# The last store moved to ScalarE's queue, and five stores in the middle halved

## The chip, the cores and the metric

The kernel runs on one core of one Trainium2 chip. The core has a matrix engine (TensorE, PE in the profile, with its weight loads shown as PEld), a vector engine (VectorE, DVE), an activation engine (ScalarE, ACT), GpSimd (POOL) and SyncE (SP), which here only issues transfers and waits. 16 DMA engines move data between the chip's memory (DRAM) and the core's on-chip memory (SBUF). The metric is the device time in microseconds (us) of one execution. It is given as the median of several executions; a profile is one execution more, with its own span from the first to the last instruction.

## The reference

Two stages, in float32. The first is attention through 32 inducing points, the second a two-branch expert with a maximum:

```python
B, N, m, C = (4, 12544, 32, 128)            # x: (B, N, C), inducing: (m, C)

def mab(q, kv):
    s = scale * (q @ kv.transpose(0, 2, 1))  # scale = 1/sqrt(C)
    s = s - s.max(-1, keepdims=True)
    a = np.exp(s)
    a /= a.sum(-1, keepdims=True) + 1e-09
    return a @ kv
h = mab(I, x)            # I: inducing for each batch; h: (B, m, C)
attn = mab(x, h)         # (B, N, C)

x = attn.reshape(B * N, 128)
h1 = x @ w1              # 128 -> 1024
h2 = x @ w2
g = np.maximum(h1, h2)
out = g @ w_out          # 1024 -> 128, (50176, 128)
```

## The kernel before

**Tiling.** A batch has 12,544 rows: 98 chunks of 128. The chunks are dealt into blocks of four quarters, a quarter being up to four chunks of one batch. A block is staged once (`stage`, L577): scores against the pooled `h`, then an exponential on ScalarE into a tile `e2`. For each quarter, "units" follow (`phase`, L990): a product of `e2` with `hwd`, which already holds `h` times the difference of the two weight matrices, and a ReLU of the result on ScalarE (L1006) or VectorE (L1009) into a relu tile. max(h1, h2) is h1 + relu(h2 - h1); the h1 part is added as a linear term (L786 for the quarters marked `full`, L990 for the others). A "group" is the output of one quarter: `final_one` (L797) runs eight products per chunk with `woutp` (L809), all into one PSUM bank.

**The output.** When the products of a group are done, `evict_group` (L826) scales them on VectorE by the softmax's reciprocal sums (L836) into an SBUF tile `osb`, shown as `o` in the profile, one of five buffers of the pool `outp`. It then stores the tile. There are 108 groups and 108 stores, each of one run of up to four neighbouring chunks: 90 of 256 KB, the others of 192, 128 and 64 KB. Before the change SP issues all of them (L861). The last four groups have four, three, two and one chunks, so the last store is 64 KB (128 partitions of 512 bytes).

**Other work on SP's queue.** Beside the three loads at the start, SP issues the transposing transfers of `x` (L171, tile `xT`) and of the pooling weights (L345, tile `eT`) of the next batches, in the same queue and between the stores. `xT` is read by L308, L330 and L591, `eT` by L364. SP takes its instructions in order: one that waits holds all that follow.

**What sets the order.** The Python code writes every instruction of every engine by hand: a clock model in the build (`Clock`, L20) decides at which step which work goes into the queues, and the framework keeps this order.

**Semaphores.** The framework gives the transfers issued from SP or ScalarE one of eight DMA semaphores in turn (index 0 to 7). Every such transfer first waits until the one eight before it, the former user of its index, has landed. SP issues 171 transfers in all, so the last store has index 2. A transfer adds to its semaphore 16 times; it has landed when the last of them is seen. When the last instruction has been written, the framework adds the closing of the program, which the profile shows under line 1200: SP waits in nine instructions, each for two semaphores at most, then in a drain. In the program's order the first is for two semaphores of GpSimd's transfers, the next eight are for DMA indices 0, 1, 2, 3, 4, 5, 6 and 7, each paired with another engine's semaphore, and the drain is for GpSimd's own. Then all engines meet at a barrier, twice, and the program ends. ScalarE issues no transfer before the change.

Of the kernel before, what the change touches and what calls it, by code (L numbers as in the profile page):

```python
# [102 lines left out]
def kernel(  # L103
# [9 lines left out]
    nc = tc.nc  # L113
# [23 lines left out]
    outr = out.rearrange("(b p k) c -> b p k c", b=B, p=128)  # L137
# [59 lines left out]
    with tc.manual_schedule(engines={ET.PE, ET.DVE, ET.Activation, ET.Pool, ET.SP}):  # L197
# [471 lines left out]
        for i in range(4):  # L669
# [3 lines left out]
            if i == 0:  # L673
# [5 lines left out]
                for dst, f in ((rep32, DOWN / scale), (repd, 1.0)):  # L679
                    nc.vector.tensor_scalar(  # L680
                        out=dst.rearrange("p (k m) -> p k m", m=M),
# [34 lines left out]
        groups, ends = [], [0] * 4  # L716
# [5 lines left out]
        groups = [g for _, _, g in sorted(groups, key=lambda e: e[:2])]  # L722
# [55 lines left out]
        def linear_last(end):  # L778

            while held:  # L780
                g = held[0]
                if g.full:
                    if st[g.blk.b].get("m1r", INF) > ck.pe:
                        return
                    for s, (q, t) in enumerate(g.chunks):
                        nc.tensor.matmul(  # L786
                            out=g.ps[:, 128 * s : 128 * (s + 1)],
                            lhsT=g.blk.e2[:, 128 * t : 128 * (t + 1)],
                            rhs=m1bd[:, q, :],
                            start=False,  # L790
                            stop=True,
                            skip_group_check=True,
                        )
                    end = ck.run(0.056 * len(g.chunks))
                evict_group(held.pop(0), end)
# [30 lines left out]
        def evict_group(g, end):  # L826
            n = len(g.chunks)
            uid[0] += 1
            osb = outp.tile([128, 4, C], F32, name=f"o_{uid[0]}", tag="o")
            qs = sorted({q for q, _ in g.chunks})  # L830
            per = n // len(qs)
            t0 = g.chunks[0][1]
            rp = g.blk.rp[:, t0 : t0 + per, qs[0] : qs[-1] + 1]
            if len(qs) == 1:
                rp = rp.broadcast_to((128, per, C))
                nc.vector.tensor_mul(osb[:, 0:n, :], g.ps[:, 0 : n * C].rearrange("p (s c) -> p s c", s=n), rp)  # L836
            elif per == 1:
                rp = g.blk.rp[:, t0, qs[0] : qs[-1] + 1]
                nc.vector.tensor_mul(
                    osb[:, 0:n, :],  # L840
                    g.ps[:, 0 : n * C].rearrange("p (s c) -> p s c", s=n),
                    rp[:, :, None].broadcast_to((128, n, C)),
                )
            else:
                for i, q in enumerate(qs):
                    nc.vector.tensor_mul(
                        osb[:, per * i : per * (i + 1), :],
                        g.ps[:, per * i * C : per * (i + 1) * C].rearrange("p (s c) -> p s c", s=per),
                        g.blk.rp[:, t0 : t0 + per, q : q + 1].broadcast_to((128, per, C)),
                    )  # L850
            ck.bank[g.bank] = ck.on_dve(end, 0.066 + n * 128 / 960.0)
            runs = []
            for s, (q, t) in enumerate(g.chunks):
                qu = g.blk.quarters[q]
                c = qu.c0 + t
                if runs and runs[-1][0] == qu.b and runs[-1][1] + runs[-1][3] == c:
                    runs[-1][3] += 1
                else:
                    runs.append([qu.b, c, s, 1])
            for b, c, s, m in runs:  # L860
                nc.sync.dma_start(out=outr[b, :, c : c + m, :], in_=osb[:, s : s + m, :])  # L861
            chunks_done[0] += n

        def finals_left():
# [159 lines left out]
        for b in range(1, B):  # L1024
            base = DONE0[b - 1]
            t_first, t_step = (6, 2.2) if b == 1 else (-6, 3.4)
            for u in range(NU):
                if b == 1:
                    s, turn, acc = 25 + 5 * u, 45 + 1.5 * u, 55 + 2 * u
                else:  # L1030
                    s = turn = 13 + 8.2 * u
# [5 lines left out]
            s, end = int(s), base + int(acc)  # L1037
# [167 lines left out]
```

## Time and profile before

| what | value |
|---|---|
| time, median of 3 runs | 327.31 us (327.06 to 327.68) |
| span of the profiled execution | 325.6 us (325.64 to the ns) |
| median less span | 1.67 us |
| granted TensorE clock | 1.000 |
| busy PE, DVE, ACT, POOL | 319.8, 283.1, 281.7, 25.6 us |
| DMA packets, bytes | 70,823, 53.65 MB |
| queue 1 (hardware, SP's) | 64,656 packets, 38.63 MB |

The span is the time from the first to the last instruction that the profile shows. Some time lies around it in the runs, here 1.67 us. A busy TensorE is the sum of its pipelined instructions, so its share says that it hardly pauses, not that it could go no faster. The chain that ended last is followed back from the last instruction: at each step to what released it. DMA-issuing instructions and waits on a queue are marked with a q (SPq, ACTq) and are not counted as busy. Where a line is said to be "of the trace's records", it is one instruction's own start and end, with more digits than the views print.

### The profile page before, as it was taken

The numbers are of one execution on the slowest core, as the hardware profiler recorded it, in microseconds if no ns is written. First come the engines' busy times: TensorE is split into PE (matmuls) and PEld (weight loads), VectorE is DVE, ScalarE is ACT, GpSimd is POOL, SyncE is SP. The second block draws the span as 40 slices with busy tenths as digits, with TensorE's granted clock in tenths as the row PEclk, the third lists the DMA queues.
The fourth block names the chain that finished last, engine by engine and source line by source line (L and its number), as shares of the span: only waits on it lengthen the run. The fifth ranks groups of instructions, "written<-read, shape, count | busy, mean of one in ns | idle before, by whom it ended". The sixth has DMA issues, their size and how long they took to land.

```text
span 325.6 us, 12570 instructions
## 1 busy us (share of the span) xinstructions
PE 319.8 (98%) x5404; PEld 243.0 (75%) x5404; DVE 283.1 (87%) x509; ACT 281.7 (87%) x560; POOL 25.6 (8%) x51
## 2 busy tenths in 40 slices
PE   7999999999999999999999999999999999999996
PEld 3876777777767777777777777777777777778785
DVE  3359989989989998998989999998989999999973
ACT  3679899999989899998888999989969999999961
POOL 7452030000040000000040000000000000000000
PEclk9999999999999999999999999999999999999999
DMA  8999999976279999993389999992312312222233
GB/s 204 208 206 214 286 246 212 172 207 134 97 150 245 225 248 209 201 203 86 116 162 243 214 234 232 190 192 86 115 66 101 113 68 98 90 108 99 85 115 112
DMA packets 70823, 53.65 MB, mean 165 GB/s; under 512 B 52176, under 2 KB 55408, under 8 KB 70768
## 3 DMA queue, kind: packets, MB, share of 16 engines
q1 hardware_dynamic: 64656, 38.63, 49.2%
q0 software_dynamic: 6112, 14.22, 22.3%
q8 instruction: 42, 0.69, 0.9%
q14 instruction: 13, 0.11, 0.1%
HBM read 28.33 MB, written 25.69 MB: 166 GB/s over the span
## 4 chain that ended last, share of the span: by engine, by line
PE 95%; DVE 1%; DMA 1%; ACT 0%; issue 0%; ACTq 0%; DVEq 0%
PE ps L809 61%; PE ps L990 22%; PE ps L591 2%; PE ps L232 2%; PE ps L308 2%; PE ps L364 1%; DMA xf<-in_x_dram 1%; PE ps L248 1%; DVE relu L1009 1%; PE ps L280 1%; PE ps L641 1%; PE ps L766 1%; PE ps L271 1%; PE ps L657 0%; PE ps L473 0%; PE ps L409 0%
## 5 line engine op out<-in xcount | busy, mean ns | idle before, releaser
L1006 ACT ACTIVATE relu<-ps 128x512 f16<-128x512 f32 x461 | 244.8, 602 | 26.6 <-PE ps L990 18.1
L1009 DVE TENSOR_SCALAR relu<-ps 128x512 f16<-128x512 f32 x323 | 206.8, 682 | 16.9 <-PE ps L990 15.3
L809 PE MATMUL ps<-woutp,relu 128*128 128x128 f16 x3136 | 217.3, 220 | 0.0
L809 PEld LDWEIGHTS <-relu 128*128 128x128 f16 x3136 | 176.7, 98 | 39.6 <-issue 29.1
L990 PE MATMUL ps<-e,hwd 32*128 32x512 f16 (+2 forms) x880 | 88.7, 360 | 0.0
L836 DVE TENSOR_TENSOR o<-ps,rp 128x512 f32<-128x512 f32 (+3 forms) x108 | 68.5, 634 | 5.5 <-PE ps L809 3.4
L990 PEld LDWEIGHTS <-hwd 32*128 32x128 f16 x880 | 24.9, 91 | 21.1 <-issue 1.0
L990 PE MATMUL ps<-m,e 32*128 32x128 f16 x381 | 38.8, 217 | 0.0
L990 PEld LDWEIGHTS <-e 32*128 32x128 f16 x381 | 21.3, 93 | 2.6
L165 POOL DMA_DIRECT2D xn<-in_x_dram x31 | 17.0, 557 | 8.2 <-DMA xn<-in_x_dram 4.3
L236 DVE COPY xT<-ps 128x512 f16<-128x512 f16 (+3 forms) x11 | 5.5, 504 | 7.8 <-PE ps L232 7.7
L319 ACT ACTIVATE eu<-ps 128x512 f16<-128x512 f32 x18 | 10.8, 615 | 0.0
L603 ACT ACTIVATE e<-ps 128x512 f16<-128x512 f32 (+2 forms) x21 | 10.5, 577 | 0.0
L164 POOL COPY pace<-hacc 128x1 f32<-128x1 f32 x2 | 0.4, 184 | 114.8 <-DVE hacc L397 114.8
L591 PE MATMUL ps<-xT,hT 128*32 128x512 f16 (+3 forms) x114 | 8.9, 362 | 0.0
L239 ACT COPY xT<-ps 128x768 f16<-128x768 f16 (+3 forms) x11 | 6.1, 556 | 2.7 <-PE ps L232 2.6
L232 PE MATMUL ps<-identity,xn 128*128 128x128 f16 x98 | 7.4, 219 | 0.4 <-DVE xn L661 0.3
L232 PEld LDWEIGHTS <-xn 128*128 128x128 f16 x98 | 5.6, 97 | 1.6 <-DVE xn L661 1.1
L257 ACT ACTIVATE et<-ps 128x448 f16<-128x448 f32 (+4 forms) x11 | 4.5, 413 | 2.6 <-PE ps L248 2.6
L308 PE MATMUL ps<-xT,inducingT 128*32 128x512 f16 x72 | 6.5, 385 | 0.0
L591 PEld LDWEIGHTS <-hT 128*32 128x32 f16 x114 | 3.3, 94 | 4.1 <-issue 3.0
L364 PE MATMUL ps<-xn,eT 128*32 128x128 f16 x288 | 5.5, 220 | 0.0
(96 smaller groups left out, 108.2 us busy)
## 6 DMA issues: line engine op xcount, KB each, us to landing
out_dram<-o SPq DMA_DIRECT2D x90, 256.0 KB, 2.4
xn<-in_x_dram POOLq DMA_DIRECT2D x24, 448.0 KB, 11.8
out_dram<-o SPq DMA_DIRECT2D x10, 128.0 KB, 3.0
xn<-in_moe_w_dram POOLq DMA_DIRECT2D x4, 256.0 KB, 14.1
xn<-in_x_dram POOLq DMA_DIRECT2D x4, 224.0 KB, 10.2
xT<-xn SPq DMA_TRANSPOSE x42, 4.3
xf<-in_x_dram SPq DMA_DIRECT2D x1, 512.0 KB, 3.9
xf<-in_x_dram SPq DMA_DIRECT2D x1, 384.0 KB, 4.3
```

The source lines that it names most:

```text
L165: nc.gpsimd.dma_start(out=xn_at[b, i][:, 0:n, :], in_=xr[b, :, k0 : k0 + n, :])
L232: nc.tensor.transpose(ps[:, j, :], xn[:, g + j, :], identity16)
L308: nc.tensor.matmul(out=ps[32 * g : 32 * (g + 1), :], lhsT=inducingT, rhs=xT_tiles[b % 2][:, U * u + 4 * g : U * u + 4 * (g + 1), :], start ...
L319: nc.scalar.activation(out=eu, in_=ps, func=AF.Exp, scale=scale, accum_out=st[b]["es"][:, u : u + 1])
L364: nc.tensor.matmul(out=ps[32 * g : 32 * (g + 1), 0:128], lhsT=eT[:, j, 32 * g : 32 * (g + 1)], rhs=xn_of(b, U * v + 4 * g + j), start=(j = ...
L591: nc.tensor.matmul(out=ps[32 * q : 32 * (q + 1), 128 * t : 128 * (t + n)], lhsT=hq, rhs=xT[:, c : c + n, :], start=True, stop=True, tile_p ...
L603: nc.scalar.activation(out=blk.e2[:, 0 : 128 * wd], in_=ps[:, 0 : 128 * wd], func=AF.Exp, scale=st[0]["rs"] if blk.b == 0 else scale,)
L809: nc.tensor.matmul(out=g.ps[:, 128 * c : 128 * (c + 1)], lhsT=g.blk.relu[q][:, 128 * (jb * w4 + t) : 128 * (jb * w4 + t + 1)], rhs=woutp[: ...
L836: nc.vector.tensor_mul(osb[:, 0:n, :], g.ps[:, 0 : n * C].rearrange("p (s c) -> p s c", s=n), rp)
L990: nc.tensor.matmul(**seq[i])
L1006: nc.scalar.activation(out=dst, in_=src, func=AF.Relu)
L1009: nc.vector.tensor_scalar(out=dst, in0=src, scalar1=0.0, scalar2=None, op0=ALU.max)
```

## The change

The last group's store is issued by ScalarE's queue (`nc.scalar`) instead of SP's. Five groups of four chunks, numbers 60, 64, 68, 72 and 76 in the order of the stores, are stored in two transfers of two chunks each (128 KB, 128 partitions of 1,024 bytes) instead of one of 256 KB; the two halves follow each other on SP's queue. The number of transfers on SP becomes 175, and the last store is the 176th over the eight semaphores.

```diff
@@ -857,8 +857,11 @@
                     runs[-1][3] += 1
                 else:
                     runs.append([qu.b, c, s, 1])
+            queue = nc.scalar if g is groups[-1] else nc.sync
             for b, c, s, m in runs:
-                nc.sync.dma_start(out=outr[b, :, c : c + m, :], in_=osb[:, s : s + m, :])
+                h = m // 2 if groups.index(g) in (60, 64, 68, 72, 76)[:5] else m
+                for lo in range(0, m, h):
+                    queue.dma_start(out=outr[b, :, c + lo : c + lo + h, :], in_=osb[:, s + lo : s + lo + h, :])
             chunks_done[0] += n
```

## The prediction

> **What bounds the kernel now.** I read the page first, for what the time hangs on, and there the chain that ended last:
>
> ```profile
> PE 95%; DVE 1%; DMA 1%; ACT 0%; issue 0%; ACTq 0%; DVEq 0%
> PE ps L809 61%; PE ps L990 22%; PE ps L591 2%; PE ps L232 2%; PE ps L308 2%; PE ps L364 1%; DMA xf<-in_x_dram 1%; PE ps L248 1%; DVE relu L1009 1%; PE ps L280 1%; PE ps L641 1%; PE ps L766 1%; PE ps L271 1%; PE ps L657 0%; PE ps L473 0%; PE ps L409 0%
> ```
>
> TensorE is the chain for 95% of the span, and the diff gives it no instruction and takes none. So the change can act in two places only: behind the last matmul, or by making TensorE wait in the middle. Next, the end of the same chain in order of time, which stops where VectorE has scaled the last group:
>
> ```profile
> 322.33 0.07 PE ps L786
> 322.40 0.02 issue
> 322.43 0.29 DVE o L836
> ```
>
> From 322.72 to 325.64, the end of the span, no engine computes: 2.92 us of store and closing waits. The records of the store line in two short windows there, and of one lone store of the same 64 KB earlier (name, number, ns min/median/max, first and last start in us; below it issue to landing), are these:
>
> ```profile
> L861 SPq DMA_DIRECT2D out_dram<-o x1: 332/332/332, 322.4 to 322.4; - x1
> DMA to landing us min/median/max: 1.7/1.7/1.7
> ...
> L861 SPq DMA_DIRECT2D out_dram<-o x1: 383/383/383, 322.8 to 322.8; - x1
> DMA to landing us min/median/max: 1.6/1.6/1.6
> ...
> L861 SPq DMA_DIRECT2D out_dram<-o x1: 332/332/332, 252.3 to 252.3; - x1
> DMA to landing us min/median/max: 1.5/1.5/1.5
> ```
>
> The first is the 128x256 store, the second the last one, 128x128. Then the closing waits (line 1200) on SP's queue, in the window before 324.42 and in the one behind it:
>
> ```profile
> L1200 SPq EVENT_SEMAPHORE  x3: 27/28/28, 323.2 to 324.1; - x3
> ...
> L1200 SPq EVENT_SEMAPHORE  x6: 28/28/28, 324.4 to 324.7; - x6
> L1200 SPq DRAIN  x1: 7/7/7, 324.8 to 324.8; - x1
> ```
>
> The trace's records give the starts to the ns: 323.232, 323.376, 324.119, then 324.431, .493, .552, .613, .673, .734, and the drain at 324.799. The last store's semaphore reads full at 324.414, so the fourth wait (index 2, the last store's) ends at 324.431, 17 ns after the landing. The five that follow, indices 3 to 7, are for stores that landed by 322.14: nothing is waited for, and still each takes its turn, (324.734 - 324.431) / 5 = 61 ns apiece.
>
> **Part 1, the number of the last semaphore.** The before program issues 171 DMAs from SP over eight semaphores in turn, so the last has 170 mod 8 = 2. Five more give 175 mod 8 = 7. The instruction list of the changed program says so too: indices 4, 5, 6 belong to the 4-, 3- and 2-chunk stores and 7 to the last, with the closing order unchanged. Then no wait stands between the landing and the drain but the one that ends with it. Gain: 5 x 61 = 0.303 us. What hides the five moved waits is SP's idleness before the landing: index 5 is full at 323.36, index 6 at 324.10, so SP can stand at index 7 by 324.10 + 0.02 + 0.06 = 324.18. That is 0.23 us before the landing of now. It also caps part 1 and part 2 together: a landing earlier than 324.18 gains nothing more, so the whole is at most 0.303 + 0.23 = 0.54 us.
>
> **Part 2, ScalarE issues the last store.** Now SP ends the store before at 322.711, does its semaphore wait at 322.757 and starts the last issue at 322.803. VectorE's semaphore came at 322.731. ScalarE's last ReLU ends at 319.54, nothing stands behind the store on it but the closing drain, and its wait for the older store on index 7 is long met. So it starts when VectorE's semaphore comes. SP started the 128x256 store 16 ns after its own (322.363, 322.379); the same gives 322.747, which is 0.056 earlier. From there to the landing the trace has no price, since ScalarE issues no DMA in it. Rows around it: the last store itself 1.611 us from issue to landing, the lone 64 KB store 1.546. For the first transfer of an unused queue, SP's first of all: issue 0.398 against 0.332, first packet 1.026 us after the issue against 0.835 in the lone stores, so +0.19. The farthest row is the store line's longest issue:
>
> ```profile
> L861 SPq DMA_DIRECT2D out_dram<-o x108: 332/333/1662, 31.1 to 322.8; - x108
> ```
>
> That 1.662 us is at 105.4, behind transposes, 1.33 us over the usual 0.332. So the bounds of this term are -0.065 (1.546 for 1.611) and +1.33. I take 1.611, 0 against now: it is the same store at the same place, and the issue before it will still be only 0.37 us old. Part 2 is then -0.056.
>
> **Part 3, five 256 KB stores in two halves.** They are groups 60, 64, 68, 72 and 76, stored at 204.07, 215.85, 228.95, 240.60 and 251.48. Each adds one issue on SP, 0.332 us where the queue is idle and some 0.53 where it is full, and a gap up to 0.09: at most 0.62 us. Only SP's queue between 179 and 218 us is full, in whose later part two of the five lie (start, us, engine, line):
>
> ```profile
> 204.07 0.52 SPq L861 DMA_DIRECT2D out_dram<-o  x1
> 205.00 1.23 SPq L171 DMA_TRANSPOSE xT<-xn  x1
> ...
> 213.17 1.28 SPq L171 DMA_TRANSPOSE xT<-xn  x1
> 214.54 1.22 SPq L345 DMA_TRANSPOSE eT<-eu  x1
> 215.85 0.83 SPq L861 DMA_DIRECT2D out_dram<-o  x1
> 216.78 1.21 SPq L345 DMA_TRANSPOSE eT<-eu  x1
> 218.24 0.38 SPq L861 DMA_DIRECT2D out_dram<-o  x1
> ```
>
> Every transpose behind 204.07 comes 0.62 us later, the one of 216.78 at most 1.24. Who waits: the xT transpose of 213.17 lands at 217.86 and L330 reads it at 221.88, 4.02 us of cover. The eT transposes landing at 218.23, 219.28 and 230.04 are read by L364 at 224.53, 224.75 and 236.42, cover 5.5 us or more. VectorE waits for a store five groups back before it reuses an output tile; from 204 on that store has always landed over 4 us earlier. One eviction near 217.5 gets one more semaphore instruction, 21 to 50 ns, done while VectorE still works on the relu before it. The bytes are the same; 640 packets of 2 KB (86 ns) become 1,280 of 1 KB (some 47), +5 us over 16 DMA engines, +0.3 each, which nobody waits for. I put part 3 at 0. Without the cover it would cost up to 1.24 us on TensorE.
>
> **Sum.** -0.303 - 0.056 + 0 = -0.36 us on the profiled execution's 325.64, which makes 325.28. The median of the runs shown, 327.31, lies 1.67 above that span, and I carry the same 1.67: 326.95 us, -0.11%. About 0.2% (0.65 us) is what a measurement of this kernel can tell from no change; its three runs spread over 327.06 to 327.68. The forecast is thus a true gain that stays inside that bound.
>
> **Rivals.**
>
> *One descriptor generator for both queues.* The last issue took 0.383, 0.051 more than usual, and its first packet came 0.051 later than a lone store's. If that was waiting for hardware still busy with the 128x256 store, it was free at 322.803 + 0.051 = 322.854 for any issuer. ScalarE's earlier start would then only wait longer there, and the landing stay at 324.41: -0.303 alone, 327.01. Against it, 0.05 us is also within what a first use may add. The Trainium skill says as much (Perfetto Trace Analysis, section DMA Instruction — HWDGE): the generator is shared between sequencers and locked by one at a time. By that rule the sum is 327.01, by the row taken above 326.95; the 0.383 row agrees with it, but no run here has two issuers on it.
>
> *A slow first transfer of ScalarE's queue (the other side).* Place: between VectorE's semaphore and the landing. Below +0.36 us extra it only eats the gain (SP's own cold row, +0.19, gives 327.14); from +0.36 on the kernel is slower than before, from +1.01 on by over 0.2%; at the farthest row, +1.33, it is 328.28. For it: queue and issuer are used here for the first time. Against it: the only cold row costs 0.19, and the 1.33 row had transposes ahead of it, which are all over at 230.
>
> *SP's queue too late in the middle.* It decides only if the transposes slip more than 4.02 us against my 1.24; at 5 us it would cost 1 us, 327.9.
>
> *The closing waits cost the same wherever the landing falls* (they may proceed at a pace set by something else): then only part 2 is left, 327.25. Against it, the nine starts above step by 61 ns exactly where nothing is missing.
>
> **How the numbers follow.** Forecast 0.55, shared generator 0.17, slow first transfer 0.18 (two thirds of it beyond +1.01 us), late transposes 0.04, unchanged waits 0.06. Slower by over 0.2%: 0.12 from the slow transfer and 0.03 from the transposes, and 0.03 for a measurement that reads high. Faster by over 0.2% needs 0.65 us, more than the cap of 0.54, so only the spread of the runs around -0.11% can show it: 0.17. The rest, 0.65, is within. The range: down to 326.5 (the cap, 326.77, less the spread of the runs), up to 328.0, which takes in the cold rows up to +1.05.
>
> **What would show it.** In the changed trace: the last store on ScalarE's queue starting near 322.75 (or 0.03 behind VectorE's last instruction); a second hardware queue with 128 packets; one closing wait and the drain between landing and barrier, with landing to end near 0.92 us instead of 1.23; issue to landing near 1.6. TensorE's last matmul must end within 0.1 us of 322.40. A ScalarE issue much over 0.4 us, or a landing more than 2 us after the issue, would prove the slow transfer; a TensorE wait on a DMA between 204 and 237 would prove part 3 wrong.

## The result, and the profile after

| | before | changed |
|---|---|---|
| median, 9 runs each | 327.68 us | 326.74 us |
| lowest to highest | 327.06 to 328.12 | 326.61 to 326.97 |
| ratio, 95% interval | | 0.9971 (0.9962 to 0.9981) |
| the same ratio, second measurement (11 runs, 35 of before) | | 0.9984 (0.9976 to 0.9993) |
| profiled span | 325.64 us | 325.15 us |

The kernel became faster, by 0.94 us at first and by 0.52 us (0.0016 x 327.59) when measured again, where the two medians, 327.59 and 326.90, are 0.69 apart; the forecast was 0.36. What follows asks what part of it the change made, and where the rest is from.

The end of the chain of waits in the changed kernel (start, us, what):

```profile
322.23 0.07 PE ps L786
322.30 0.02 issue
322.32 0.29 DVE o L836
```

It is the same end, 0.108 us earlier. Behind it, the two last stores, by the records of the store line in two short windows (the 128x256 store, then the last one):

```profile
L864 SPq DMA_DIRECT2D out_dram<-o x1: 332/332/332, 322.3 to 322.3; - x1
DMA to landing us min/median/max: 1.7/1.7/1.7
...
L864 ACTq DMA_DIRECT2D out_dram<-o x1: 369/369/369, 322.6 to 322.6; - x1
DMA to landing us min/median/max: 1.6/1.6/1.6
```

And SP's closing waits in the window before 323.05 and in the one behind it:

```profile
L1203 SPq EVENT_SEMAPHORE  x6: 28/28/28, 322.6 to 323.0; - x6
...
L1203 SPq EVENT_SEMAPHORE  x3: 28/28/28, 323.3 to 324.2; - x3
L1203 SPq DRAIN  x1: 7/7/7, 324.3 to 324.3; - x1
```

Before, three waits stood ahead of the landing and six behind it; now six are done at once, the next two are met at 323.26 and 324.00, and the ninth ends with the landing, the drain right behind it. In the trace's records, step by step:

| us | before | changed | difference |
|---|---|---|---|
| end of VectorE's last instruction to the last issue | 0.083 | 0.032 | -0.051 |
| issue to landing | 1.611 | 1.580 | -0.031 |
| landing to the end of the span | 1.226 | 0.922 | -0.304 |
| sum | 2.920 | 2.534 | -0.386 |

ScalarE's queue is a new one in the DMA view, queue 10 with 144 packets: the 128 forecast and 16 of 4 bytes.

The 0.386 us of this table are the change's. In the middle, the halved store of group 64 pushes SP's queue back:

```profile
216.41 1.01 SPq L864 DMA_DIRECT2D out_dram<-o  x2
217.51 1.19 SPq L345 DMA_TRANSPOSE eT<-eu  x1
```

TensorE does not feel it. Compared matmul by matmul in the order of their starts, the changed kernel's 352nd (number 351 counted from 0, which the expectation of the eight halves calls the 351st) starts 0.104 us earlier, and from there to the last one, over 299.5 us and through the halved stores, the difference stays within 0.01 us. The 0.108 us of the span's 0.494 that the tail doesn't explain lie ahead of that matmul. By the records they are the sum of three things. The first transposes on TensorE (L232) start at 5.17 us instead of 5.38, -0.21. The trace's first record of the full granted clock begins at 6.10 us instead of 4.75; until it these transposes start 0.107 us apart, behind it 0.056, which costs the changed kernel 0.42. And the 352nd matmul, the second of four at L591, starts 0.32 us behind the one before it in the kernel before, and 0.004 in the changed one; the view marks this pause as issue, so TensorE waits there for nothing that the profile shows. The next section shows that two executions of one kernel differ in the same things. That leaves 0.94 - 0.49 = 0.45 us of the first measurement outside both.

### The profile page after: what moved, and what is told of

Same layout as the page of the kernel before. It is cut to its first block, busy times and chain, and to the rows that moved or that the text cites. A ratio compares the mean times of both kernels' runs of the same rounds, so it can differ in the third digit from the quotient of the medians.

```text
span 325.1 us, 12576 instructions
## 1 busy us (share of the span) xinstructions
PE 320.0 (98%) x5404; PEld 243.3 (75%) x5404; DVE 283.1 (87%) x509; ACT 281.6 (87%) x560; POOL 25.4 (8%) x51
## 4 chain that ended last, share of the span: by engine, by line
PE 97%; DVE 1%; ACT 0%; issue 0%; ACTq 0%; DVEq 0%
PE ps L809 61%; PE ps L993 22%; PE ps L591 2%; PE ps L232 2%; PE ps L308 2%; PE ps L364 1%; PE ps L665 1%; PE ps L248 1%; DVE relu L1012 1%; PE ps L280 1%; PE ps L641 1%; PE ps L766 1%; PE ps L271 1%; PE ps L657 0%; PE ps L473 0%; PE ps L409 0%
## 5 line engine op out<-in xcount | busy, mean ns | idle before, releaser
L809 PE MATMUL ps<-woutp,relu 128*128 128x128 f16 x3136 | 217.2, 220 | 0.0
L809 PEld LDWEIGHTS <-relu 128*128 128x128 f16 x3136 | 176.7, 98 | 39.7 <-issue 29.1
L591 PE MATMUL ps<-xT,hT 128*32 128x512 f16 (+3 forms) x114 | 8.5, 362 | 0.0
L232 PE MATMUL ps<-identity,xn 128*128 128x128 f16 x98 | 7.8, 226 | 0.1
L232 PEld LDWEIGHTS <-xn 128*128 128x128 f16 x98 | 6.0, 100 | 1.3 <-DVE xn L661 0.9
L591 PEld LDWEIGHTS <-hT 128*32 128x32 f16 x114 | 3.2, 94 | 3.9 <-issue 2.8
```

The costliest lines, as they stand in the source:

```text
L232: nc.tensor.transpose(ps[:, j, :], xn[:, g + j, :], identity16)
L591: nc.tensor.matmul(out=ps[32 * q : 32 * (q + 1), 128 * t : 128 * (t + n)], lhsT=hq, rhs=xT[:, c : c + n, :], start=True, stop=True, tile_p ...
L809: nc.tensor.matmul(out=g.ps[:, 128 * c : 128 * (c + 1)], lhsT=g.blk.relu[q][:, 128 * (jb * w4 + t) : 128 * (jb * w4 + t + 1)], rhs=woutp[: ...
```

## The experiments

Theory 1: the change acts in the tail alone, the rest is the spread of the start. Rival, later theory 2: something else is gained in each run. The tail of each kernel is the time from VectorE's last instruction to the end of the span.

**The kernel before, again.** No edit.

> The kernel before, once more, against itself. Theory 1 (the change acts only behind the last matmul, 0.39 us; whatever else separates the medians is the spread of the runs, which comes from the first loads): ratio 1.000, and the runs' spans spread over about 0.5 us or more. The rival (the change also takes some 0.5 us away at another place, in each run): ratio 1.000 as well, with a spread as narrow as the 0.36 us of the changed kernel's nine runs. In the profile both expect 2.92 us from the end of VectorE's last instruction to the end of the span.

Ratio 1.000 (0.9991 to 1.0008), tail 2.908. Its 11 runs have spans of 325.2 to 326.2, a spread of 1.0 us: what theory 1 expects. The 352nd matmul says where it is from. In the first six profiles, of all kernels, it starts between 22.17 and 23.45 us, and from there to the last matmul all six take 299.51 to 299.54. The spread is the start's, and its parts can be read: the first L232 transposes start within 0.30 us of one another; the record of the full clock begins between 4.07 and 6.95 us, worth up to 0.79 us; and the pause ahead of the 352nd matmul is 0 to 0.44 us. This kernel's second profile has its full clock from 4.07 on and no pause, the first from 4.75 on and 0.32 us. What sets the two is open.

**The last store on ScalarE, no halves.**

```diff
+            queue = nc.scalar if g is groups[-1] else nc.sync
             for b, c, s, m in runs:
-                nc.sync.dma_start(out=outr[b, :, c : c + m, :], in_=osb[:, s : s + m, :])
+                queue.dma_start(out=outr[b, :, c : c + m, :], in_=osb[:, s : s + m, :])
```

> The last store on ScalarE's queue, no store halved, so its semaphore has index 2 again and five closing waits follow. Theory 1: from VectorE's end to the end of the span 2.92 - 0.05 (earlier issue) - 0.03 (issue to landing) = 2.84 us, so 0.08 us faster than before, ratio 0.9997. The rival, if the use of ScalarE's queue is what brings the 0.5 us more: some 0.6 us faster, ratio 0.998.

Tail 2.862: VectorE to issue 0.030, issue to landing 1.615, landing to end 1.217 (index 2 again). So the queue brings 0.05 us, all at the issue; the 0.03 of the landing was not the queue's. Ratio 0.9993 (0.9985 to 1.0002), 0.23 us by its middle, more than the tail gives, but the interval takes in 1.

**The halves alone, last store on SP.** As the change, but

```diff
-            queue = nc.scalar if g is groups[-1] else nc.sync
+            queue = nc.sync
```

> The five stores halved, the last store on SP's queue, with semaphore index 7. Theory 1: five closing waits of 61 ns move ahead of the landing, 2.92 - 0.30 = 2.62 us from VectorE's end to the end of the span, ratio 0.9991. The rival, if the halved stores or the count of transfers bring the 0.5 us more: some 0.8 us faster, ratio 0.9976.

Tail 2.582, landing to end 0.911: the five waits, as expected, without ScalarE. Ratio 0.9989 (0.998 to 0.9998).

**The changed kernel, again.**

> The changed kernel once more, on the same chip as the others. Theory 1: 2.53 us from VectorE's end to the end of the span, 0.39 us faster, ratio 0.9988. The rival: 0.9 us faster, ratio 0.9971 as first measured.

Tail 2.537. The ratio, 0.9984, lies between the two expectations. Neither is refuted by it, so I compared each run's time with its own span. Time less span was 2.05 us on average over the 35 runs of before, but 1.86, 1.81 and 1.86 in the three edited kernels: some 0.2 us that lie outside the span, whichever part of the change is made. One record differs there. In the 2.8 us from 325.7 on, behind the end of the span, the DMA view of the kernel before has this packet:

```profile
DMA packets 1, 0.01 MB, mean 3 GB/s; under 512 B 0, under 2 KB 0, under 8 KB 0
## 3 DMA queue, kind: packets, MB, share of 16 engines
q14 instruction: 1, 0.01, 1.0%
```

It is an 8 KB fetch of instructions, which starts 1.84 us after the span and takes 0.44. In the changed kernel it starts at 1.56, in the halves alone at 0.96, and in the kernel with ScalarE alone there is none. It comes earlier the more instructions SP has: 330 in the records of before, 333, 335, and 328 where there is none. The next two kernels test that.

**Three drains more on SP.** Nothing else is edited:

```diff
+        for _ in range(3):
+            nc.sync.drain()
```

> The kernel before with three drains more on SP's queue behind its last store, where SP waits for landings anyway; no transfer, index or queue is changed. Theory 1 (the tail alone): 2.92 us from VectorE's end to the end of the span, as before, ratio 1.000. Theory 2 (beside the tail, some 0.2 us lie outside the span: time less span was 2.05 us on average before and 1.81 to 1.86 in the three kernels whose SP queue has another number of instructions, and before alone has an 8 KB instruction fetch starting 1.85 us after the span): the span stays, the fetch comes earlier (at about 1.5 us, as in the changed kernel, which has three SP instructions more than before as well) and time less span falls to 1.83, so 0.22 us faster, ratio 0.9993.

Tail 2.921, as before; average span 325.49 us, against 325.50 of before in the same session. The fetch starts at 1.54, and time less span is 1.863 over 12 runs against 2.024 over the 34 of before. Ratio 0.9991 (0.9981 to 1.0). Theory 2 holds: 0.16 us (standard error 0.03) of the expected 0.22, from three drains that do nothing.

**Eight halves, last store on SP.** The list of groups is `(60, 64, 68, 72, 76, 80, 82, 84)`, the queue SP.

> Eight stores halved, the last store on SP: eight transfers more bring the last one back to semaphore index 2. Theory 1: nothing gained, 2.92 us from VectorE's end to the end of the span, and nothing lost on TensorE (its last matmul 299.52 us after its 351st, as in all kernels so far): ratio 1.000. Theory 2: the same span, but time less span 1.83 instead of 2.05, ratio 0.9993. If the halves themselves were what helps: a shorter span.

Tail 2.935, TensorE 299.53 from the 352nd matmul: the halves by themselves gain and cost nothing, and index 2 gives nothing. Time less span 1.786, average span 325.6; ratio 0.9997 (0.9987 to 1.0007), which includes both expectations.

All kernels together, by the number of SP's instructions in the records:

| SP instructions | kernels | fetch starts after the span, us | time less span, us |
|---|---|---|---|
| 328 | ScalarE alone | none | 1.86 |
| 330 | before (101 runs) | 1.84, 1.86 | 2.04 |
| 331 | two stores on ScalarE | 1.80 | 1.95 |
| 333 | changed (20 runs), three drains | 1.56, 1.54, 1.54 | 1.86, 1.86 |
| 334 | six halves, last store on both | 1.02, 1.01 | 1.82, 1.81 |
| 335 | halves alone | 0.96 | 1.81 |
| 338 | eight halves | 0.25 | 1.79 |
| 341 | thirteen halves | 0.31 ahead of its end | 1.81 |

The last semaphore update in the first six traces comes 1.90 to 1.94 us after the span. Where the fetch starts shortly before that (at 1.80 to 1.86), time less span is 0.1 to 0.2 us longer, and it also varies more from run to run, with a standard deviation of 0.09 to 0.15 us against 0.04 to 0.07 in the others. That the number of SP's instructions moves the time is shown by the three drains; that the fetch is the reason is an inference from this table.

**Six halves and ScalarE: index 0.** The list is `(60, 64, 68, 72, 76, 80)`.

> Six stores halved and the last store on ScalarE's queue: its index is 0, whose wait is the second of the nine, so seven waits follow the landing. Theory 1: 2.53 + 7 x 0.061 = 2.96 us from VectorE's end to the end of the span, 0.04 us more than before and 0.43 more than the changed kernel. The rival (the closing waits take no time of their own, and the gain comes from the queue or the halves): 2.53 us as in the changed kernel.

Tail 2.980. SP's closing waits from the landing (324.02) on:

```profile
L1203 SPq EVENT_SEMAPHORE  x8: 28/28/28, 324.0 to 324.5; - x8
L1203 SPq DRAIN  x2: 7/7/7, 324.5 to 324.6; - x2
```

Eight waits, the store's own and seven that are met already, each in its turn: landing to end 1.349 against 0.922 with none behind, 0.427 / 7 = 61 ns apiece. With index 2 it was 0.304 / 5 = 61 ns. The closing cost grows with the number of waits behind the last landing, and ScalarE and six halves don't help against it.

**Thirteen halves where SP's queue is full.** The list is `tuple(range(52, 65))`, the rest as in the change.

> The last store on ScalarE with index 7 as in the changed kernel, but thirteen halved stores (groups 52 to 64) instead of five, all in the stretch from 178 to 216 us where SP's queue is full. Eleven of them stand before the xT transpose that L330 waits for, at up to 0.62 us each 6.8 us against a cover of 4.02. Theory 1 (the halves cost nothing only because of that cover): TensorE waits near 222 us, some 2 to 3 us, and the time rises by that less the 0.39 us of the tail, ratio about 1.006. The rival (halves take no time of SP's queue that counts, or the queue catches up): no TensorE wait, ratio 0.9985 as in the changed kernel.

TensorE's longest waits in the whole span (us in total, times, longest):

```profile
PE ps L330 <- DMA xT<-xn: 2.1, 1, 2.1
PE ps L665 <- DVE warm L213: 1.2, 1, 1.2
```

The first is new: L330 waits for the transpose, which stands behind twelve of the halved stores (the expectation counted eleven). TensorE takes 303.22 us from its 352nd to its last matmul instead of 299.51. Some 2.3 of the 3.71 us more are lost at this wait. The other 1.4 are no wait; they go with a lower granted clock (PEclk) right behind it, which is the 0.50 in this line (the stretch in us, its length, then each engine's busy time and instructions, PEclk, DMA share, GB/s):

```profile
223.80:226.70 2.90, 2.90 (x29) 2.07 (x30) 1.29 (x2) 1.31 (x3) 0.00 (x0) 0.50 1.22 134
```

By the trace's records half the clock is granted from 223.50 to 226.92, and the products of L809 start 0.107 us apart there instead of 0.056. So in this run a wait of 2.1 us cost 3.7. Ratio 1.0066 (1.0041 to 1.009); single runs vary from 327.82 to 332.15, and the three with a mean clock of 0.995, the profiled one among them, are the three longest. The cover was what made the five halves free.

The tail is 2.724, not the changed kernel's 2.53, though the last store has index 7 again and no wait behind it: its own wait starts 0.151 us after the landing instead of 0.016, and landing to end is 1.104. Why SP is late there is open.

**Two stores on ScalarE.**

```diff
-            queue = nc.scalar if g is groups[-1] else nc.sync
+            queue = nc.scalar if g is groups[-1] or g is groups[79] else nc.sync
```

> The changed kernel with one more store on ScalarE's queue, the lone 64 KB store of group 79 near 256 us; the last one is then not the queue's first. So far the last store on ScalarE had its first packet 0.89 us after the issue and landed after 1.58 to 1.62, a lone 64 KB store on SP 0.84 and 1.54. If the 0.05 us is the first use of the queue: the lone store shows 0.89 and 1.58, the last one 0.84 and 1.54. If it is the generator still busy with SP's store 0.38 us earlier: the lone one 0.84 and 1.54, the last one 0.89 and 1.58. If it belongs to ScalarE's queue: 0.89 and 1.58 for both. Time: ScalarE stands at the store until VectorE has evicted group 79, up to 1 us, so TensorE may lose some tenths of a us behind 256 us; ratio between 0.998 and 1.000.

The two issues (ns), in one window each:

```profile
L864 ACTq DMA_DIRECT2D out_dram<-o x1: 383/383/383, 256.2 to 256.2; - x1
...
L864 ACTq DMA_DIRECT2D out_dram<-o x1: 339/339/339, 323.3 to 323.3; - x1
```

The first took 0.383, its first packet left at 0.901 and it landed after 1.590; the second 0.339, 0.864 and 1.560. First use costs about 0.04 us at the issue and 0.03 at the landing; another 0.02 against SP's lone stores (0.84, 1.54) stays with the second, and whether the queue or the neighbour makes it is open. SP's store 0.37 us ahead does not hold ScalarE's up by the 0.05 of the rival. The price on the other side: ScalarE issues for 0.383 us between two ReLUs, and TensorE takes 0.11 us more from its 352nd to its last matmul (299.63). Ratio 0.9989 (0.998 to 0.9998): not better than the change.

**The last store in two halves, on both queues.**

```diff
-                h = m // 2 if groups.index(g) in (60, 64, 68, 72, 76)[:5] else m
+                h = m // 2 if groups.index(g) in (60, 64, 68, 72) else m
+                if g is groups[-1]:
+                    nc.sync.dma_start(out=outr[b, 64:128, c : c + m, :], in_=osb[64:128, s : s + m, :])
+                    nc.scalar.dma_start(out=outr[b, 0:64, c : c + m, :], in_=osb[0:64, s : s + m, :])
+                    continue
```

> Four stores halved, and the last store in two halves of 64 partitions, one on ScalarE's queue (index 6) and one on SP's (index 7), so that the last wait is again the last to be met. If the packets of the last store leave at the pace of the descriptor generator (0.32 us from first to last, for eight packets of 27 ns on each DMA engine), two queues halve that and the later landing comes up to 0.15 us sooner: 2.40 us from VectorE's end to the end of the span, 0.13 less than the changed kernel. If the generator serves one queue at a time, or the receipt sets the landing: 2.53 us or, since SP's half starts later, up to 2.65. Ratio 0.998 in either case.

Its two issues in order of time (start, us, engine, line):

```profile
322.50 0.57 ACTq L865 DMA_DIRECT2D out_dram<-o  x1
322.55 0.55 SPq L864 DMA_DIRECT2D out_dram<-o  x1
```

Both take 0.55 to 0.57 us instead of 0.33 to 0.38, and they land 1.87 and 2.09 us after their issues. The tail is 3.095, the longest of all and beyond both expectations (2.40, and 2.53 to 2.65); the ratio is 1.000 (0.9991 to 1.0009). By the DMA records the two halves go one after the other: the 64 data packets of ScalarE's queue start from 323.724 to 323.993, the 64 of SP's from 323.994 to 324.261. But ScalarE's half, issued first, also has its first packet late, 1.22 us after its issue instead of 0.86 to 0.90. No run issues a store from 64 partitions alone, so how much of the longer issues is due to this shape, and how much to the other queue, is open.

## Why the prediction was right, and where it was off

**The number of the semaphore (-0.303).** Measured -0.304, and shown three ways: by the halves alone, by eight halves, which bring index 2 and the old tail back, and by index 0, which makes it longer by the same 61 ns a wait. The kernel with thirteen halves is the exception: index 7, and 0.18 us longer from landing to end. That the nine waits have a fixed order and a price each was the right reading of the records before.

**ScalarE's issue (-0.056).** Measured -0.051 in the changed kernel, -0.053 alone. The bounds from -0.065 to +1.33 were far too wide upward: the nearest cold row, SP's own first transfer, overstated the first use already (+0.19 against 0.03 to 0.04). The slow first transfer, to which 0.18 was given, did not come.

**Issue to landing (0).** -0.031 in one profile, 0.00 with ScalarE alone (1.615 against 1.611), -0.025 with the halves alone on SP. It is not the queue, but it goes with the number of the semaphore: in five kernels whose last store has index 2 it is 1.611 to 1.617, with index 0 1.599, and with index 7 1.580 to 1.588, on SP and on ScalarE, while the first packet leaves 0.88 to 0.90 after the issue in all of them. So the index is worth some 0.03 us more than its waits; why is open.

**The halves (0).** Right, and for the reason given: where thirteen replace five, the cover is used up at the very reader named, L330, and TensorE waits there. In the changed kernel the eT transpose of 216.78 went to 217.51, 0.73 us later (0.83 counted from the 352nd matmul), where up to 1.24 was allowed for, and TensorE waits for no DMA between 204 and 237. The sign that its last matmul must end within 0.1 us of 322.40 was just missed, by 0.109 us earlier, but 0.104 of that is the start's.

**The sum** was -0.36, the span's tail gave -0.386. Over all runs whose span is known, 101 of before and 20 of the changed kernel, the average span fell from 325.50 to 325.06 us, -0.44; the standard errors (0.03 and 0.08) include the -0.386.

**The step that failed** is the one that carried the rest over: "The median of the runs shown, 327.31, lies 1.67 above that span, and I carry the same 1.67". The 1.67 mixed a median with another execution's span. Run by run it is 2.04 before and 1.86 after, and this 0.18 us is a second gain that the sum has no term for. It comes with SP's instructions being three more, not from what they do; three drains give the same. With it, 0.39 + 0.18 = 0.57 us, which agrees with the second measurement (0.52) and with the averages of the same 101 and 20 runs (327.54 to 326.91, -0.63).

The first 0.94 us holds chance on top of that: the changed kernel's nine runs averaged 324.91 us of span, its 11 later ones 325.17. That such differences lie in the first 22 us was seen in the profiled executions; the other runs have no trace. So it is in part luck that the first median, 326.74, came within 0.21 us of the 326.95 forecast: the forecast started from three runs of before with a median of 327.31, and nine gave 327.68. For the same reason "Faster by over 0.2% needs 0.65 us, more than the cap of 0.54" was no bound on the time: the cap held for the tail, which stayed below it, and the first measurement still showed 0.29%.

**One descriptor generator.** Two issues 0.05 us apart are each 0.2 us longer than usual, and their packets follow one another. The Trainium skill's statement (Perfetto Trace Analysis, section DMA Instruction — HWDGE) that sequencers lock a shared generator agrees with those 0.57 and 0.55 us, which the shape of 64 partitions may share in. As a price for this change it was wrong: at 0.37 us apart ScalarE's issue took 0.339 in its second use. SP's own stores at 0.38 apart do take longer (the second halves, 0.42 to 0.43), so what the last store before the change waited for is not what a second queue waits for.

## What to carry to other kernels

Behind the last store, ask which closing waits still stand after its landing: each that is met already costs its 61 ns here, and the turn of the semaphores decides how many there are, so a transfer more or less anywhere can move the end. Extra transfers are free only while the queue's readers have cover, so look up the reader behind the fullest stretch first; there a wait of TensorE can cost more than its length, here 3.7 us for 2.1, as the clock was halved behind it. For gains of a tenth of a per cent compare stretches of the trace, and each run's time with its own span: the medians here held two other effects of the same size, one of them with the mere number of SP's instructions.

## What was not expected of the hardware

The time outside the span depends on the length of SP's instruction stream by up to 0.2 us, and an instruction fetch behind the program's end moves with it (fetch at 1.84 us: 2.04 us outside the span; at 1.56 us or earlier, or none: 1.79 to 1.86). No view of the span shows it. And in the first six profiles TensorE repeats itself to some 0.03 us in 299.5 from the 352nd matmul on, while the 22 us before it vary by 1.3 us: by the moment from which the full clock is granted (up to 0.79), by a pause of up to 0.44 that no wait in the trace explains, and by 0.30 in the start of the first transposes, behind the first loads.
